# Two query-weight loads moved to SyncE's queue, one MLP copy moved to VectorE, ScalarE's small operations held back by a stricter test, and a late normalisation put ahead of a fold

## The chip, the core and the metric

One core of a Trainium2 chip runs the whole program. Its engines work side by side: TensorE (PE in the profile; PEld is its loading of weights), VectorE (DVE), ScalarE (ACT), GpSimd (POOL) and SyncE (SP). SyncE computes nothing and issues transfers; GpSimd and ScalarE issue transfers too. The transfers themselves run on 16 DMA engines. In the profile, queue q1 carries what SyncE issues, q10 what ScalarE issues and q0 what GpSimd issues; q8 and q14 bring instructions. The metric is device time in microseconds (us), lower is better.

## What is computed

A layer-normalised input of 2048 tokens and 512 channels goes through two branches, an attention with 32 heads over cached keys and values and an MLP of two stages. The attention's output, gated by the MLP's, is added to the input:

```python
xn = _layernorm(x, axis=-1)
s = _A_ref(xn, A_k_cache, A_v_cache, A_wq, A_wo)
g = _silu(_B_ref(xn, B_w1, B_w2, B_w3, B_w4))
return x + s * g
```

`_A_ref` forms queries `x @ wq`, scores against `k_cache` (32 heads, 2048 keys, 128 channels), a softmax, the product with `v_cache`, and the product with `wo`. `_B_ref` forms `gelu(layernorm(x) @ w1)`, shifts its four channel groups by one or two tokens, multiplies by `w2`, adds `x`, and then runs `gelu(layernorm(.) @ w3) @ w4`.

## The kernel before

**Units and slots.** Attention is cut into 128 units: 8 groups of 4 heads, in each group 4 query tiles of 512 tokens, in each tile the 4 heads (`units`). A unit has 8 slots (`SPU`), and slot n of the program is slot `p = n % 8` of unit `u = n // 8`. In every slot TensorE makes two score products of 512 columns (`s_slot`, into `ps_s`, of which there are two buffers), ScalarE takes their exponential in one instruction of 128x1024 (L222, into `pT`), and some slots later TensorE multiplies an earlier `pT` with the values (`pv_slot`, into `ps_o`, two buffers). Four products a slot are the base load. The other products are spread over the slots: the next queries (`q_mm`, in slots 0 and 1), the output projection (`wo_mm`, slots 4 and 5), and the MLP (slots 2, 3, 6 and 7). All engines run their instructions in the order in which this loop writes them (`pin`).

**VectorE** sums each unit's exponentials (`add_first` L228, `add_next` L233), folds the sum (`fold`, L237 and L238), forms the reciprocal, and multiplies `ps_o` with it (`norm`, L305), which also frees that `ps_o` buffer. In units after `LATE` = 20 the normalisation of unit u-3 stands in slot 1 of unit u (`normed(u - 3)`). For units that are not `turned` (the first four and the last two) the fold of unit u-1 is written in slot 0 and its sum is taken by TensorE (`sums`, four one-column products); for all others it is in slot 2, and the sum goes through a DMA transpose.

**ScalarE's small operations.** A chunk of the MLP's first stage ends with a copy of `ps_m` to `pre` (L591), on ScalarE. Two copies make a pair for `gelu_pair`: two squares (L550), a polynomial on VectorE (L554), two hyperbolic tangents (L559) and a last product on VectorE (L562). Squares and tangents wait in the list `act_late`, and at most one of them is written at the end of a slot. A budget decides which: `debt[0]` grows by `SMALL` = 2.4 (in units of one product's time) for each small operation and by `EXP_OVER` = 0.2 for each slot, and shrinks by the extra products of the slot; an operation is written when `debt[0] + SMALL` is at most what the next two slots bring in extra products (`ahead`). MLP chunks run from unit 5 on; `wo_todo` is the list of output projections that are due.

**The start.** Unit 0 is done in halves (`first_tokens`): token tiles are turned by TensorE, the first queries formed, and four half-size exponentials (L513) taken, with the queries of units 1 and 2 in between. Before that the loads are written in this order: x on SyncE and ScalarE; the query weights of heads 0, 1 and 2 on GpSimd (`load_w`, 128 KB each); on SyncE the keys of head 0 in four quarters (`load_k`, a DMA transpose of 128 KB each, L173), the values of head 0 in two halves (`load_v`, 256 KB each, L183), the four quarters of head 1's keys, and then head 2's; on GpSimd the fourth query weights, four more tiles of x, and the values of head 1. A score slot p reads quarter p // 2 of its head's keys, so unit 1 (slots 8 to 15) wants its first quarter in slot 8 and its second in slot 10. All SyncE's transfers stand in one queue in order of issue.

Of the kernel before, what the change touches and what calls it, by code (L numbers as in the profile page):

```python
# [8 lines left out]
ACT = mybir.ActivationFunctionType  # L9
ALU = mybir.AluOpType  # L10
# [7 lines left out]
def kernel(  # L18
# [15 lines left out]
    nc = tc.nc  # L34
# [16 lines left out]
    HG = 4 if H % 4 == 0 else (2 if H % 2 == 0 else 1)  # L51
    NG = H // HG

    SPU = KC // 2
    LAG = 4
    KSPLIT = 4
# [6 lines left out]
    pin = tc.keep_in_program_order  # L63

    def pool(name, bufs=1, space=None, **kw):
# [22 lines left out]
        out=ident[:], in0=diag[:], scalar1=0.0, scalar2=None, op0=ALU.is_equal))  # L88
# [30 lines left out]
    debt = [0.0]  # L119
    SMALL = 2.4  # L120
    EXP_OVER = 0.2

    def mm(out, lhsT, rhs, start, stop):
        mm_count[0] += out.shape[-1] / 512
        pin(nc.tensor.matmul(out=out, lhsT=lhsT, rhs=rhs, start=start, stop=stop))  # L125
# [24 lines left out]
    LATE = 20  # L150
# [6 lines left out]
    def at(n, fn):  # L157
        todo[n].append(fn)
# [9 lines left out]
    def load_k(h, pieces):  # L168
        w = Sk // KSPLIT
        for i in pieces:  # L170
            if i == 0:
                kTs[h] = kp.tile([P, Sk], BF16, name="kT")
            pin(nc.sync.dma_start(  # L173
                out=kTs[h][:, i * w:(i + 1) * w],
                in_=A_k_cache[0, h, i * w:(i + 1) * w, :], transpose=True))

    def load_v(h, halves, eng=nc.sync):
        v = A_v_cache[0, h].rearrange("(i p j) d -> p i j d", p=P, j=KJ)
        for i in halves:
            if i == 0:  # L180
                vBs[h] = vp.tile([P, KC, Dh], BF16, name="vb")
            ks = slice(i * KSPLIT // 2, (i + 1) * KSPLIT // 2)
            pin(eng.dma_start(  # L183
                out=vBs[h].rearrange("p (i j) d -> p i j d", j=KJ)[:, ks], in_=v[:, ks]))

    def load_w(h, eng=nc.sync):
        wqs[h] = wqp.tile([P, DC, Dh], BF16, name="wq_h")
        pin(eng.dma_start(out=wqs[h][:], in_=wq_v[:, :, h * Dh:(h + 1) * Dh]))
# [42 lines left out]
    def add_next(u, i):  # L231
        a = st[u]["acc"]
        pin(nc.vector.tensor_tensor(out=a[:], in0=a[:], in1=st[u]["pT"][i][:], op=ALU.add))  # L233

    def fold(u):
        a = st[u]["acc"]
        pin(nc.vector.tensor_tensor(out=a[:, 0:2, :], in0=a[:, 0:2, :], in1=a[:, 2:4, :], op=ALU.add))  # L237
        pin(nc.vector.tensor_tensor(out=a[:, 0, :], in0=a[:, 0, :], in1=a[:, 1, :], op=ALU.add))  # L238
# [26 lines left out]
    def turned(u):  # L265
        return T0 <= u < T1
# [275 lines left out]
    mlp = {}  # L542
    act_late = deque()

    def gelu_pair(pre, dest, n):
        sq = gtp.tile([P, 2, 512], BF16, name="sq")
        f2 = "p a f -> p (a f)"

        def square(a):
            pin(nc.scalar.activation(  # L550
                out=sq[:, a, :], in_=pre[:, a, :], func=ACT.Square, scale=GELU_A ** 0.5))

        def poly():
            pin(nc.vector.scalar_tensor_tensor(  # L554
                out=sq[:].rearrange(f2), in0=sq[:].rearrange(f2), scalar=1.0,
                in1=pre[:].rearrange(f2), op0=ALU.add, op1=ALU.mult))

        def tanh(a):
            pin(nc.scalar.activation(out=sq[:, a, :], in_=sq[:, a, :], func=ACT.Tanh, scale=GELU_C))  # L559

        def last():
            pin(nc.vector.scalar_tensor_tensor(  # L562
                out=sq[:] if callable(dest) else dest, in0=sq[:], scalar=1.0, in1=pre[:],
                op0=ALU.add, op1=ALU.mult))

        def squared(n):
            square(1)
            k = soft(n + 1)
            at(k, poly)
            at(k + 2, lambda: act_late.extend((lambda n: tanh(0), tanhed)))  # L570

        def tanhed(n):
            tanh(1)
            k = soft(n + 2)
            at(k, last)
            if callable(dest):
                for a in range(2):
                    at(k + 2 + a, lambda a=a: dest(sq[:, a, :], a))

        act_late.extend((lambda n: square(0), squared))  # L580

    def gelu_chunk(lhs, rhs, j, scale, dest):
        def run(i, n):
            if i == 0:
                mlp["ps"] = psX.tile([P, 512], FP32, tag="xm", name="ps_m")
            mm(mlp["ps"][:], lhs(i), rhs(i), i == 0, i == DC - 1)
            if i == DC - 1:
                if j == 0:
                    mlp["pre"] = gtp.tile([P, 2, 512], BF16, name="pre")
                pre = mlp["pre"]  # L590
                pin(nc.scalar.activation(out=pre[:, j, :], in_=mlp["ps"][:], func=ACT.Identity,  # L591
                                         **({} if scale is None else dict(scale=scale))))
                debt[0] += SMALL
                if j == 1:
                    gelu_pair(pre, dest(), n)
        run.size = DC
        return run
# [186 lines left out]
    wo_todo = deque()  # L784

    def ahead(n):
        u, p = divmod(n, SPU)
        if p in (2, 3, 6, 7):
            return window[p % 2] if p % 2 and window else 1 if chunks and u >= W0 // 2 else 0
        if p in (4, 5) and u < 4 * HG and not wo_todo:  # L790
            return 0
        return 2
# [3 lines left out]
        ln1_load(t, eng)  # L796
    act1 = const.tile([P, 1], FP32, name="act1")
    pin(nc.scalar.activation(out=act1[:], in_=nhalf[:, 0:1], func=ACT.Identity))
    for h in range(HG - 1):
        load_w(h, nc.gpsimd)  # L800
    load_k(0, range(KSPLIT))
    load_v(0, (0, 1))
    load_k(1, range(KSPLIT))
    warm_up(WARM)
# [28 lines left out]
    for g in range(NG - 1):  # L833
        b = (g * QT + QT - 1) * HG
        for hh in range(HG):
            h = (g + 1) * HG + hh
            for i in range(KSPLIT):
                n = (b - 2 + (2 * hh + i // 2 + (hh > 0))) * SPU + (5, 7)[i % 2]
# [22 lines left out]
    def normed(u):  # L861
        norm(u)
        gg, qq, hh = units[u]
        if hh == HG - 1 and (gg, qq) in deferred:
            at((u + 4) * SPU + 4, lambda: pin(nc.sync.dma_start(out=o_d[(gg, qq)][:], in_=oTs[(gg, qq)][:])))
        elif hh == HG - 1:
            wo_todo.extend((gg, 4 * qq + ts) for ts in range(4))
            if gg == NG - 1:
                fin_load(4 * qq)

    for n in range(NS):
        u, p = divmod(n, SPU)
# [23 lines left out]
            turned_sums(u - 2)  # L896
        if p == 0 and u >= 1:
            add_next(u - 1, 3)
            if not turned(u - 1):
                fold(u - 1)  # L900
        if p == (1 if mlp.get("stage") == 2 or u >= QUIET else 2) and HG < u < NU - 2:
            q_copy(u + 2)
# [3 lines left out]
            acc_turn(u - 1)  # L906
        if p == 1 and u > LATE:
            normed(u - 3)
        if p == (3 if u >= LATE else 2) and u >= 2 and turned(u - 2):
            bcast(u - 2)  # L910
        if n in norms:
# [44 lines left out]
            fn()  # L956
        x = mm_count[0] - mm_before - 4
        debt[0] = max(0.0, debt[0] + EXP_OVER - x) if n >= HALF else 0.0
        if act_late and debt[0] + SMALL <= ahead(n + 1) + ahead(n + 2):
            act_late.popleft()(n)  # L960
            debt[0] += SMALL
        if p == SPU - 1 and u >= 2 and turned(u - 2) and (u < LATE or u == NU - 1):
# [57 lines left out]
    for i, queue in enumerate((nc.sync, nc.scalar)):  # L1020
        cs = slice(i * D // 2, (i + 1) * D // 2)
        ps = halves[i][:, cs]
# [36 lines left out]
```

## Time and profile before

| | us |
|---|---|
| three runs: median (lowest to highest) | 1247.22 (1245.70 to 1248.73) |
| the profiled execution: its own time | 1247.53 |
| the profiled execution: its span | 1245.7 |
| TensorE busy | 1232.4 (99%) |
| ScalarE busy | 1129.2 (91%) |
| VectorE busy | 1116.5 (90%) |
| GpSimd busy | 174.6 (14%) |
| exponentials of 128x1024 (L222), each | 1.029 |
| copies `pre<-ps_m` with a scale (L591), median of 16 | 0.69 |

The span runs from the first instruction to the last; the execution's own time is 1.8 us longer, for what lies around it. A product of 512 columns is listed with 0.38 us, but products are pipelined and follow each other at 0.22 us, so TensorE's busy share tells only where it stood still for longer than that overlap. "Idle before" counts time in which an engine did nothing, and the arrow names what ended it. In the table of windows "x" counts the instructions that began in the stretch, and the DMA share is the mean over 16 engines. A few records of products are missing from the trace.

### The profile page before, as it was taken

The page shows a single profiled execution, that of the slowest core. Times are in us where ns is not written, and L with a number is a line of the kernel's source. Part 1 is how long each engine was busy: PE and PEld are TensorE (multiplying, and loading weights), DVE is VectorE, ACT ScalarE, POOL GpSimd, SP SyncE. Part 2 cuts the span into 40 slices and gives each one's busy share as a digit, 9 for nine tenths or more (in the row PEclk, how much of TensorE's full clock was granted, in tenths as well). Part 3 has the DMA queues.
Part 4 walks back from the last instruction along what each step waited for, and adds up shares of the span by engine and source line. Part 5 has one row for each costly group of instructions (what it writes and reads, how often), then busy time and mean ns, then how long its engine had stood idle before and what let it go on. Part 6 is the DMA issues. An engine that isn't in the chain of part 4 may idle for free.

```text
span 1245.7 us, 16531 instructions
## 1 busy us (share of the span) xinstructions
PE 1232.4 (99%) x5702; PEld 597.1 (48%) x5816; DVE 1116.5 (90%) x1520; ACT 1129.2 (91%) x1285; POOL 174.6 (14%) x301
## 2 busy tenths in 40 slices
PE   8999999999999999999999999999999999999998
PEld 5444444444444444444444444444444444444444
DVE  6999999999999988899988889999888999888998
ACT  8999999888999888899988889998888999988992
POOL 6563003432111000000100000010000000000110
PEclk9999999999999999999999999999999999999999
DMA  9565573665634455233484235734446233563464
GB/s 196 127 112 105 98 145 76 127 132 113 143 72 106 110 102 119 48 95 75 104 151 93 68 77 108 134 75 84 85 98 127 56 89 65 123 144 74 105 146 113
DMA packets 248404, 131.42 MB, mean 105 GB/s; under 512 B 200000, under 2 KB 224960, under 8 KB 248320
## 3 DMA queue, kind: packets, MB, share of 16 engines
q1 hardware_dynamic: 238752, 103.94, 40.1%
q0 software_dynamic: 8992, 25.96, 9.4%
q8 instruction: 45, 0.74, 0.3%
q14 instruction: 39, 0.32, 0.1%
q10 hardware_dynamic: 576, 0.46, 0.1%
HBM read 83.62 MB, written 8.13 MB: 74 GB/s over the span
## 4 chain that ended last, share of the span: by engine, by line
PE 93%; DVE 3%; DMA 2%; ACT 1%; SPq 1%; issue 1%; DVEq 0%; ACTq 0%
PE ps_o L125 34%; PE ps_s L125 33%; PE ps_m L125 10%; PE ps_q L125 8%; PE ps_wo L125 8%; DMA kT<-in_A_k_cache_dram 1%; ACT pT L222 1%; DVE acc L233 1%; SPq L173 0%; DVE acc L228 0%; DVE oT L305 0%; DMA rb<-dr 0%; DMA wo<-in_A_wo_dram 0%; DVE acc L237 0%; DVE bn L414 0%
## 5 line engine op out<-in xcount | busy, mean ns | idle before, releaser
L222 ACT ACTIVATE pT<-ps_s 128x1024 bf16<-128x1024 f32 x1020 | 1017.9, 1029 | 90.8 <-PE ps_s L125 75.0
L125 PE MATMUL ps_o<-pT,vb 128*128 128x512 bf16 x2027 | 602.9, 379 | 3.8 <-DVE oT L305 0.2
L125 PE MATMUL ps_s<-qT,kT 128*128 128x512 bf16 (+1 forms) x1992 | 595.3, 378 | 3.3 <-DMA kT<-in_A_k_cache_dram 1.8
L125 PEld LDWEIGHTS <-kT 128*128 128x128 bf16 x2056 | 232.5, 113 | 228.5 <-DMA kT<-in_A_k_cache_dram 2.5
L233 DVE TENSOR_TENSOR acc<-acc,pT 128x2048 bf16<-128x2048 bf16 x256 | 310.5, 1213 | 15.1 <-ACT pT L222 13.7
L125 PEld LDWEIGHTS <-vb 128*128 128x128 bf16 x2048 | 200.3, 98 | 225.8 <-issue 0.5
L228 DVE TENSOR_TENSOR acc<-pT 128x2048 bf16<-128x2048 bf16 x128 | 156.2, 1220 | 31.1 <-ACT pT L222 30.6
L125 PE MATMUL ps_q<-xnT,wq_h 128*128 128x512 bf16 (+1 forms) x517 | 151.3, 374 | 0.5
L125 PE MATMUL ps_wo<-wo_h,oT 128*128 128x512 bf16 (+1 forms) x453 | 133.6, 377 | 0.2
L305 DVE TENSOR_TENSOR oT<-ps_o,rb 128x512 bf16<-128x512 f32 x122 | 130.9, 1073 | 2.9 <-DMA rb<-dr 2.7
L391 DVE TENSOR_TENSOR s_acc<-ps_wo,s_acc 128x512 f32<-128x512 f32 x96 | 66.0, 688 | 41.1 <-PE ps_wo L125 40.4
L237 DVE TENSOR_TENSOR acc<-acc 128x1024 bf16<-128x1024 bf16 x128 | 87.5, 683 | 0.3
L276 DVE TENSOR_REDUCE sm<-accT 128x4 f32<-128x512 bf16 x122 | 82.7, 678 | 2.6 <-DMA accT<-acc 2.6
L125 PEld LDWEIGHTS <-wq_h 128*128 128x128 bf16 x524 | 50.7, 98 | 59.5 <-issue 0.4
L208 DVE CAST qT<-ps_q 128x512 bf16<-128x512 f32 x109 | 75.0, 688 | 3.2 <-PE ps_q L125 2.9
L125 PE MATMUL ps_m<-xn2T,w_sb 128*128 128x512 bf16 x218 | 75.3, 379 | 0.1
L125 PE MATMUL ps_m<-w_sb,h2T 128*128 128x512 bf16 x218 | 75.3, 379 | 0.1
L723 POOL DMA_DIRECT2D w_sb<-in_B_w_dram x28 | 21.2, 756 | 371.9 <-PE ps_m L125 309.9
L125 PEld LDWEIGHTS <-oT 128*128 128x128 bf16 x468 | 45.7, 98 | 54.5 <-DVE oT L312 0.3
L751 POOL DMA_DIRECT2D g_d<-xr x16 | 8.8, 548 | 438.2 <-DVE xr L749 438.2
L238 DVE TENSOR_TENSOR acc<-acc 128x512 bf16<-128x512 bf16 x128 | 54.4, 425 | 4.4
L554 DVE SCALAR_TENSOR_TENSOR sq<-sq,pre 128x1024 bf16<-128x1024 bf16 x36 | 44.0, 1222 | 4.7 <-ACT sq L550 4.6
(102 smaller groups left out, 635.3 us busy)
## 6 DMA issues: line engine op xcount, KB each, us to landing
rb<-dr SPq DMA_DIRECT2D x127, 256.0 KB, 3.8
vb<-in_A_v_cache_dram SPq DMA_DIRECT2D x60, 256.0 KB, 3.9
w_sb<-in_B_w_dram POOLq DMA_DIRECT2D x28, 256.0 KB, 4.2
wo_h<-in_A_wo_dram SPq DMA_DIRECT2D x32, 128.0 KB, 3.5
wq_h<-in_A_wq_dram SPq DMA_DIRECT2D x28, 128.0 KB, 3.2
kT<-in_A_k_cache_dram SPq DMA_TRANSPOSE x128, 3.7
dr<-rc SPq DMA_DIRECT2D x128, 2.0 KB, 2.2
xr<-in_A_x_dram POOLq DMA_DIRECT2D x16, 128.0 KB, 3.1
```

Source lines behind the costliest of these rows:

```text
L125: pin(nc.tensor.matmul(out=out, lhsT=lhsT, rhs=rhs, start=start, stop=stop))
L208: pin(nc.vector.tensor_copy(out=qT[:], in_=st[u].pop("psq")[:]))
L222: pin(nc.scalar.activation(out=s["pT"][-1][:, jj:jj + 2, :], in_=sps[:], func=ACT.Exp, scale=SCALE))
L228: pin(nc.vector.tensor_tensor(out=s["acc"][:], in0=s["pT"][0][:], in1=s["pT"][1][:], op=ALU.add))
L233: pin(nc.vector.tensor_tensor(out=a[:], in0=a[:], in1=st[u]["pT"][i][:], op=ALU.add))
L237: pin(nc.vector.tensor_tensor(out=a[:, 0:2, :], in0=a[:, 0:2, :], in1=a[:, 2:4, :], op=ALU.add))
L238: pin(nc.vector.tensor_tensor(out=a[:, 0, :], in0=a[:, 0, :], in1=a[:, 1, :], op=ALU.add))
L276: pin(nc.vector.tensor_reduce(out=sm[:], in_=s.pop("at")[:], axis=mybir.AxisListType.X, op=ALU.add))
L305: pin(nc.vector.tensor_tensor(out=oTs[(g, qt)][:, hh, :].rearrange(f, j=4), in0=s["o"].rearrange(f, j=4), in1=s["rb"].rearrange("x (p j) - ...
L391: pin(nc.vector.tensor_tensor(out=sa, in0=ps[:], in1=sa, op=ALU.add))
L554: pin(nc.vector.scalar_tensor_tensor(out=sq[:].rearrange(f2), in0=sq[:].rearrange(f2), scalar=1.0, in1=pre[:].rearrange(f2), op0=ALU.add, ...
L723: pin(nc.gpsimd.dma_start(out=w[:], in_=w3_v[:, :, fc * P:(fc + 2) * P]))
```

## The change

Four edits, in the program's order of lines.

```diff
@@ gelu_chunk: the copy at the end of an MLP chunk
-                pin(nc.scalar.activation(out=pre[:, j, :], in_=mlp["ps"][:], func=ACT.Identity,
-                                         **({} if scale is None else dict(scale=scale))))
-                debt[0] += SMALL
+                if scale is not None and n % SPU == 3 and not wo_todo:
+                    pin(nc.vector.tensor_scalar(
+                        out=pre[:, j, :], in0=mlp["ps"][:], scalar1=scale, scalar2=None, op0=ALU.mult))
+                else:
+                    pin(nc.scalar.activation(out=pre[:, j, :], in_=mlp["ps"][:], func=ACT.Identity,
+                                             **({} if scale is None else dict(scale=scale))))
+                    debt[0] += SMALL
@@ the first loads
-    for h in range(HG - 1):
-        load_w(h, nc.gpsimd)
-    load_k(0, range(KSPLIT))
+    load_w(0, nc.gpsimd)
+    load_k(0, (0, 1))
+    for h in range(1, HG - 1):
+        load_w(h)
+        load_k(0, (h + 1,))
     load_v(0, (0, 1))
     load_k(1, range(KSPLIT))
@@ the loop over slots: slot 0
             add_next(u - 1, 3)
-            if not turned(u - 1):
+            if not turned(u - 1) and u <= LATE:
                 fold(u - 1)
@@ the loop over slots: slot 1
         if p == 1 and u > LATE:
             normed(u - 3)
+            if not turned(u - 1):
+                fold(u - 1)
@@ the loop over slots: end of a slot
-        if act_late and debt[0] + SMALL <= ahead(n + 1) + ahead(n + 2):
+        if act_late and debt[0] + SMALL + 2 * EXP_OVER <= ahead(n + 1) + ahead(n + 2):
             act_late.popleft()(n)
             debt[0] += SMALL
```

TensorE's order of instructions is the same in both programs. Of the 72 copies of `ps_m`, the condition holds for one, the copy of token tile 5 in slot 75, in unit 9; on VectorE it stands behind the fold of unit 8 and ahead of the first sum of unit 9. The stricter test moves 21 of 72 squares and 11 of 72 tangents, each by one slot; of VectorE's last products four move behind two more instructions, the others stay. The moved fold is met once, in the last unit.

**SyncE at the start.** Its rows before; `kT` are a head's keys, `vb` its values, `wq_h` query weights, `xnT` turned tokens:

```order
L408 DMA xin<-in_A_x_dram 128x512 x2
L173 DMA_TRANSPOSE kT<-in_A_k_cache_dram 128x512 x4
L183 DMA vb<-in_A_v_cache_dram 128x2x512 x2
L173 DMA_TRANSPOSE kT<-in_A_k_cache_dram 128x512 x8
L465 DMA_TRANSPOSE xnT<-xn 128x4x128
L173 DMA_TRANSPOSE kT<-in_A_k_cache_dram 128x512
```

and now:

```order
L408 DMA xin<-in_A_x_dram 128x512 x2
L173 DMA_TRANSPOSE kT<-in_A_k_cache_dram 128x512 x2
L188 DMA wq_h<-in_A_wq_dram 128x4x128
L173 DMA_TRANSPOSE kT<-in_A_k_cache_dram 128x512
L188 DMA wq_h<-in_A_wq_dram 128x4x128
L173 DMA_TRANSPOSE kT<-in_A_k_cache_dram 128x512
L183 DMA vb<-in_A_v_cache_dram 128x2x512 x2
L173 DMA_TRANSPOSE kT<-in_A_k_cache_dram 128x512 x8
L465 DMA_TRANSPOSE xnT<-xn 128x4x128
```

Two loads of 128 KB now stand ahead of the third and fourth quarter of head 0's keys, and so ahead of head 0's values and of head 1's keys (the first four of the row of eight). GpSimd's row of three such loads is now a row of one; the rest of its start is the same.

**ScalarE in slot 51 and after**, at the end of the second chunk of the MLP. Before:

```order
L591 ACTIVATE pre<-ps_m,mvA 128x512
L550 ACTIVATE sq<-pre 128x512
L222 ACTIVATE pT<-ps_s 128x1024 x3
L550 ACTIVATE sq<-pre 128x512
L222 ACTIVATE pT<-ps_s 128x1024
L591 ACTIVATE pre<-ps_m,mvA 128x512
```

and now:

```order
L595 ACTIVATE pre<-ps_m,mvA 128x512
L222 ACTIVATE pT<-ps_s 128x1024
L550 ACTIVATE sq<-pre 128x512
L222 ACTIVATE pT<-ps_s 128x1024 x2
L550 ACTIVATE sq<-pre 128x512
L222 ACTIVATE pT<-ps_s 128x1024
L595 ACTIVATE pre<-ps_m,mvA 128x512
```

A copy and a square that followed each other now have an exponential between them. The same happens in slots 63, 103, 115 and 127, and in later ones.

**VectorE in unit 127**, slots 0 to 2 (`acc` is a unit's sum of exponentials, `oT` its normalised output, `gl` and `xl` the last steps of an output tile):

```order
 L261 RECIPROCAL rc<-sm 128x4
 L233 TENSOR_TENSOR acc<-acc,pT 128x2048
-L237 TENSOR_TENSOR acc<-acc 128x1024
-L238 TENSOR_TENSOR acc<-acc 128x512
-L305 TENSOR_TENSOR oT<-ps_o,rb 128x512
+L305 TENSOR_TENSOR oT<-ps_o,rb 128x512
+L237 TENSOR_TENSOR acc<-acc 128x1024
+L238 TENSOR_TENSOR acc<-acc 128x512
 L396 SCALAR_TENSOR_TENSOR gl<-s_acc,gl 128x512
 L398 TENSOR_TENSOR xl<-gl,xl 128x512
```

The normalisation of unit 124 now stands ahead of the two folds of unit 126.

## The prediction

> **What bounds the kernel now.** I read the page first, then the windows, the waits, the chain of waits, and the timeline where those point.
>
> ```profile
> PE 1232.4 (99%) x5702; PEld 597.1 (48%) x5816; DVE 1116.5 (90%) x1520; ACT 1129.2 (91%) x1285; POOL 174.6 (14%) x301
> PE 93%; DVE 3%; DMA 2%; ACT 1%; SPq 1%; issue 1%; DVEq 0%; ACTq 0%
> ```
>
> TensorE is busy for 99% of the span and holds 93% of the chain. Its products are not changed, so only its standstills can be won or lengthened, and the windows say where they are:
>
> ```profile
> 15.00:20.00 5.00, 3.44 (x17) 1.50 (x16) 4.90 (x9) 3.99 (x5) 4.76 (x6) 1.00 0.64 111
> 100.00:150.00 50.00, 49.73 (x227) 23.75 (x231) 46.76 (x59) 49.29 (x63) 5.74 (x8) 1.00 0.54 101
> 1050.00:1100.00 50.00, 49.74 (x228) 24.01 (x232) 43.98 (x57) 46.07 (x50) 1.08 (x2) 1.00 0.55 122
> ```
>
> The columns are PE, PEld, DVE, ACT and POOL, then clock, DMA share and GB/s. From 100 us on, 231 or 232 weight loads pass in every 50 us, one per 0.216 us, at full clock: TensorE runs at its rate, and work moved on other engines changes nothing there unless it makes TensorE wait. Only 15 to 20 us shows a hole. The waits name it:
>
> ```profile
> PEld L125 <- DMA kT<-in_A_k_cache_dram: 2.5, 2, 2.1
> PE ps_s L125 <- DMA kT<-in_A_k_cache_dram: 1.8, 2, 1.6
> ```
>
> Two waits for keys, the longer 1.6 us of idle PE. The chain shows whose keys:
>
> ```profile
> 7.96 1.15 SPq L173
> 9.15 10.72 DMA kT<-in_A_k_cache_dram
> ```
>
> SyncE's issue at 7.96 is the first quarter of head 1's keys; the second, issued at 9.15, landed 10.72 us later, at 19.87. On the timeline of PE and of ACT:
>
> ```profile
> 17.76 0.59 PE L125 MATMUL ps_o<-pT,vb 128*128 128x512 bf16 x2
> 19.92 0.63 PE L125 MATMUL ps_s<-qT,kT 128*128 128x512 bf16 x2 [1.56 <-DMA kT<-in_A_k_cache_dram]
> 14.18 4.81 ACT L222 ACTIVATE pT<-ps_s 128x1024 bf16<-128x1024 f32 x5
> 20.58 1.94 ACT L222 ACTIVATE pT<-ps_s 128x1024 bf16<-128x1024 f32 x2 [1.59 <-PE ps_s L125]
> ```
>
> Two products after 17.76 the next was due at 18.19 and began at 19.92, 1.73 us late. ScalarE, with one exponential per 0.96 us behind products that need 0.86, is the slower one here; it was free at 18.99 and idle for 1.59. So 1.59 us is what the absence of this wait is worth.
>
> **The change part by part.** *Loads.* Each weight load costs SyncE one issue:
>
> ```profile
> L188 SPq DMA_DIRECT2D wq_h<-in_A_wq_dram x26: 426/526/595, 112.9 to 1044.3; - x26
> ```
>
> With the 0.04 us between issues, two take 1.13 us, so head 1's second quarter is issued at 10.28, not 9.15. Its landing after the change is in no trace. The nearest rows are the first quarter's and the second's own:
>
> ```profile
> DMA to landing us min/median/max: 6.1/6.1/6.1
> ```
>
> This is the transfer issued at 7.96: 6.1 us. With 6.1 the second quarter would land at 16.4, ahead of its use; with 10.72 at 21.0. The difference between the two is a stop of the DMA engines, seen in the window from 14 to 18 us in 40 slices:
>
> ```profile
> DMA  9999090000002000200010101010110000093909
> q0 software_dynamic: 85, 0.28, 92.3%
> q1 hardware_dynamic: 524, 0.13, 20.3%
> q8 instruction: 1, 0.02, 1.7%
> ```
>
> From 14.5 to 17.5 almost no packet starts. GpSimd's queue q0 has packets open throughout (92.3%), SyncE's q1 hardly, and one instruction fetch (q8) falls into it. TensorE's program is the same, so I expect the fetch and the stop to stay, and what is open at 14.5 to land after 17.5. What changes is how much stands behind: q0 carries 256 KB less at the start, so head 1's values on it are further by then, and q1 carries 256 KB more. The bounds are the whole wait gone, and 10.72 us counted from the later issue. The small wait ahead of it goes too if head 0's second quarter no longer shares with those loads:
>
> ```profile
> 10.54 1.02 ACT L513 ACTIVATE pT<-ps_s 128x1024 bf16<-128x1024 f32 x1 [0.26 <-PE ps_s L125]
> ```
>
> It is worth 0.26, and only if the later wait does not swallow it. So the edit lies between -1.85 (1.59 + 0.26) and +1.13. The middle is -0.4; I take **-0.6**, towards the gain, because a quarter that is open when the stop ends has fewer packets of q0 to share with. Head 1's weights are read just ahead of the exponential at 10.54; if they came 1 us late, the wait at 19.92 would take that in.
>
> *ScalarE's stricter test.* Where a copy and a square stand together, the next exponential is late and with it the free `ps_s` buffer:
>
> ```profile
> 63.13 0.63 ACT L550 ACTIVATE sq<-pre 128x512 bf16<-128x512 bf16 x1
> 63.65 1.94 ACT L222 ACTIVATE pT<-ps_s 128x1024 bf16<-128x1024 f32 x2
> 64.25 0.59 PE L125 MATMUL ps_wo<-wo_h,oT 128*128 128x512 bf16 x2
> 64.73 0.59 PE L125 MATMUL ps_s<-qT,kT 128*128 128x512 bf16 x2
> ...
> 156.29 0.59 PE L125 MATMUL ps_q<-xnT,wq_h 128*128 128x512 bf16 x2
> 156.77 0.59 PE L125 MATMUL ps_s<-qT,kT 128*128 128x512 bf16 x2
> ```
>
> Two products take 0.43, these starts lie 0.48 apart: 0.05 lost. Slots 51, 63, 103, 115 and 127 have that pair, and each is followed by one such start, the first and the last shown: 5 x 0.05 = **-0.25**. The later moves fall where the windows show TensorE at its rate, and gain nothing. What is made later is covered: all moved squares are the first of their pair, so the polynomial, which needs the second, stays; the four last products that move are read by TensorE seven or more slots on. Bounds: -0.3, and +0.25 if as many new late starts appear one slot on.
>
> *The copy on VectorE.* Slot 75:
>
> ```profile
> 91.80 0.69 ACT L591 ACTIVATE pre<-ps_m,mv 128x512 bf16<-128x512 f32 x1
> 92.38 2.84 ACT L222 ACTIVATE pT<-ps_s 128x1024 bf16<-128x1024 f32 x3
> 92.83 0.59 PE L125 MATMUL ps_o<-pT,vb 128*128 128x512 bf16 x2
> 93.45 0.59 PE L125 MATMUL ps_s<-qT,kT 128*128 128x512 bf16 x2
> 94.34 1.23 DVE L233 TENSOR_TENSOR acc<-acc,pT 128x2048 bf16<-128x2048 bf16 x1 [1.08 <-ACT pT L222]
> 90.39 0.68 DVE L208 CAST qT<-ps_q 128x512 bf16<-128x512 f32 x1
> ```
>
> Without the copy the exponential starts 0.58 earlier, and the scores start at 93.26 (92.83 + 0.43), not 93.45: **-0.19**. VectorE's copy has no row; its cast from the same kind of buffer takes 0.68. It delays the first sum behind it by some 0.6, which the idle 1.08 ahead of 94.34 takes in. Were that gone, the sums and then the normalisation would be 0.6 late: up to +0.2 after the 0.19 given up.
>
> *Fold after normalisation, last unit.*
>
> ```profile
> 1217.54 0.42 DVE L238 TENSOR_TENSOR acc<-acc 128x512 bf16<-128x512 bf16 x1
> 1217.88 1.07 DVE L305 TENSOR_TENSOR oT<-ps_o,rb 128x512 bf16<-128x512 f32 x1
> 1218.22 0.59 PE L125 MATMUL ps_s<-qT,kT 128*128 128x512 bf16 x2
> 1218.99 0.59 PE L125 MATMUL ps_o<-pT,vb 128*128 128x512 bf16 x2 [0.18 <-DVE oT L305]
> 1219.42 0.27 PE L125 MATMUL ps_sum<-ones_t,acc 128*128 128x1 bf16 x4
> L295 SPq DMA_DIRECT2D rb<-dr x1: 1299/1299/1299, 1212.0 to 1212.0; - x1
> DMA to landing us min/median/max: 4.6/4.6/4.6
> ```
>
> The product on `ps_o` was due at 1218.65 and began at 1218.99, 0.34 late, behind the normalisation that frees the buffer. Ahead of the two folds that one starts 1.07 earlier, near 1216.8; its factors, issued at 1212.0, landed after 4.6 us (the last two rows), at 1216.6, just in time. The folds then end near 1218.95, and the sum's products want them at 1219.08: close, so **-0.3** of the 0.34. Bounds -0.34 and 0.
>
> *Sum:* -0.6 - 0.25 - 0.19 - 0.3 = -1.3. The profiled execution (span 1245.7) took 1247.53, 0.3 above the median 1247.22; from it 1246.2, from the median 1245.9. I write 1246.0.
>
> **The rivals.** *A, the wait for keys goes altogether.* For it: the first quarter needed 6.1 us under the same load, and q0 is relieved. Against: the stop. -1.85 - 0.74 = -2.6, 1244.6. Chance 0.28.
>
> *B, slower: head 1's keys come later still.* They stand behind 256 KB more in SyncE's queue, and the DMA engines are slow while both queues feed them, as from 4 to 9 us:
>
> ```profile
> DMA packets 1648, 0.71 MB, mean 142 GB/s; under 512 B 1566, under 2 KB 1566, under 8 KB 1648
> ```
>
> 256 KB at 142 GB/s are 1.8 us, with the later issue up to 2.9; if the first quarter, wanted two slots earlier, meets the stop and the second comes 5 us behind it as before, some 4. After the 0.74 of the small edits: +1.1 to +3.3, 1248.3 to 1250.5. It decides from a landing after 20.6; beyond 0.2% from 23.1. Chance 0.25.
>
> [...]
>
> *C, the small edits do not do what they say:* late starts return a slot on and the sums wait for the folds; with the loads at -0.3, 1246.9. Chance 0.08.
>
> **How the numbers follow.** The forecast has 0.39, A 0.28, B 0.25, C 0.08. The forecast's own range is 1245.0 to 1247.0; the runs before spread by 1.5 to each side. The range runs from 1243.9 (A, with spread) to 1249.2 (B's middle). 0.2%, about what a measurement of this kernel can tell from no change, is 2.5 us: faster by more is some 0.7 of A and a little of the forecast, 0.25; slower by more is 0.6 of B, 0.15; the rest, 0.60, lies between.
>
> **What would show it.** In the changed kernel's trace: the wait for `kT` near 19.9 shorter and the loads right; gone, A; longer, or a new one two slots ahead of it, B. Starts at 64.7 and 156.8 that lie 0.43 behind the products before them; the one at 93.4 too; no `[... <-DVE oT L305]` near 1219 and no wait of `ps_sum`. A stop of the DMA engines that is not there at all, or a new wait in the 1000 us in which TensorE ran at its rate, would make this wrong.

## The result and the profile after

| | before | after |
|---|---|---|
| median of 10 runs each, same chip (lowest to highest), us | 1246.44 (1245.40 to 1248.73) | 1249.56 (1248.28 to 1253.40) |
| ratio with its 95% interval | | 1.0028 (1.0020 to 1.0036) |
| the profiled execution, us | 1247.53 | 1253.40 |
| its span, us | 1245.7 | 1251.6 |

The change makes the kernel 0.28% slower, above the predicted range. Rival B happened. The execution profiled after the change is the slowest of its ten, so its pieces are larger than those of a usual run; a second profile below shows how much.

The page's first row and its chain by engine, of the kernel after:

```profile
PE 1241.1 (99%) x5816; PEld 598.8 (48%) x5816; DVE 1117.1 (89%) x1521; ACT 1129.0 (90%) x1284; POOL 173.5 (14%) x299
PE 98%; DMA 1%; SPq 1%; DVE 0%; issue 0%
```

The waits (us in total, times, longest):

```profile
PE ps_s L125 <- DMA kT<-in_A_k_cache_dram: 5.1, 1, 5.1
```

One wait for keys of 5.1 us, where there were two, the longer 1.6. The chain of waits says which keys:

```profile
4.20 0.58 SPq L188
...
9.05 12.70 DMA kT<-in_A_k_cache_dram
```

The two moved loads (L188; the second is issued at 6.06) now stand in the chain of SyncE's issues, and behind them head 1's first quarter is issued at 9.05 and lands 12.70 later. Before, it was issued at 7.96 and landed after 6.1. PE's timeline:

```profile
16.15 0.59 PE L125 MATMUL ps_o<-pT,vb 128*128 128x512 bf16 x2
21.79 1.04 PE L125 MATMUL ps_s<-qT,kT 128*128 128x512 bf16 x2 [5.05 <-DMA kT<-in_A_k_cache_dram]
22.63 1.06 PE L125 MATMUL ps_o<-pT,vb 128*128 128x512 bf16 x2
```

Slot 8, which began at 16.25 before, begins at 21.79. After that two products take 0.84, not 0.43. The windows show why (the columns are as in the prediction):

```profile
15.00:20.00 5.00, 1.74 (x9) 0.62 (x6) 4.90 (x8) 2.42 (x3) 4.80 (x6) 1.00 0.66 68
20.00:25.00 5.00, 3.21 (x8) 1.21 (x9) 2.17 (x6) 1.02 (x1) 3.73 (x9) 0.57 1.13 287
25.00:30.00 5.00, 5.00 (x22) 2.17 (x21) 0.35 (x2) 3.96 (x4) 0.39 (x1) 0.75 1.02 237
```

The granted clock is 0.57 and 0.75 in the ten us that follow, in windows of 1 us 0.50 from 21 to 27; from 30 us on it is 1.00 again. The same product began at 59.94 before and at 66.43 after:

```profile
66.43 0.59 PE L125 MATMUL ps_s<-qT,kT 128*128 128x512 bf16 x2
```

These 6.5 us are 5.54 for slot 8, less the 1.73 by which slot 10 was late before, and a rest of 2.7. The low clock is large enough for this rest: the two windows withhold 0.43 and 0.25 of 5 us, 3.4 us in all, a part of it while TensorE still stood (an estimate). The last product ends 5.5 us later, so the rest of the program gave some 0.9 back. Places of the small edits, in order: the pair in slot 51, the pair in slot 127, the last unit:

```profile
70.75 0.59 PE L125 MATMUL ps_wo<-wo_h,oT 128*128 128x512 bf16 x2
71.18 0.59 PE L125 MATMUL ps_s<-qT,kT 128*128 128x512 bf16 x2
...
162.39 0.59 PE L125 MATMUL ps_q<-xnT,wq_h 128*128 128x512 bf16 x2
162.82 0.59 PE L125 MATMUL ps_s<-qT,kT 128*128 128x512 bf16 x2
...
1224.52 0.59 PE L125 MATMUL ps_o<-pT,vb 128*128 128x512 bf16 x2
1224.95 0.28 PE L125 MATMUL ps_sum<-ones_t,acc 128*128 128x1 bf16 x4
```

The scores start 0.43 behind the products before them, not 0.48, and the last unit has no wait for `oT`. The small edits do what they were said to do; the loss is at the start.

### The profile page after: what moved, and what is told of

Read it like the earlier page. It is cut to its first block, busy times and chain, and to the rows that moved or that the text cites. A ratio compares the mean times of both kernels' runs of the same rounds, so it can differ in the third digit from the quotient of the medians.

```text
span 1251.6 us, 16646 instructions
## 1 busy us (share of the span) xinstructions
PE 1241.1 (99%) x5816; PEld 598.8 (48%) x5816; DVE 1117.1 (89%) x1521; ACT 1129.0 (90%) x1284; POOL 173.5 (14%) x299
## 3 DMA queue, kind: packets, MB, share of 16 engines
q1 hardware_dynamic: 239808, 104.20, 40.5%
q0 software_dynamic: 8896, 25.70, 9.3%
## 4 chain that ended last, share of the span: by engine, by line
PE 98%; DMA 1%; SPq 1%; DVE 0%; issue 0%
PE ps_s L125 36%; PE ps_o L125 35%; PE ps_m L125 10%; PE ps_q L125 9%; PE ps_wo L125 8%; DMA kT<-in_A_k_cache_dram 1%; SPq L173 0%; SPq L188 0%; SPq L183 0%; SPq L408 0%; PE ps_sum L125 0%; DVE gf L368 0%; DVE xf L373 0%
## 5 line engine op out<-in xcount | busy, mean ns | idle before, releaser
L125 PE MATMUL ps_s<-qT,kT 128*128 128x512 bf16 (+1 forms) x2056 | 610.6, 379 | 5.1 <-DMA kT<-in_A_k_cache_dram 5.1
```

## The experiments

A 95% interval stands behind every ratio to the kernel before, which ran beside each group of kernels on the same chip. The groups ran on different chips, and there the kernel before has medians from 1245.8 to 1247.8, so two ratios compare well only within a group: e1 to e4, e5 to e8, e9 to e12, e13 alone, e14 and e15.

### Which edit

**The loads alone**, and **all but the loads**:

```diff
# e1: the kernel before, with
+    load_w(0, nc.gpsimd)
+    load_k(0, (0, 1))
+    for h in range(1, HG - 1):
+        load_w(h)
+        load_k(0, (h + 1,))
# e2: the changed kernel, with
+    for h in range(HG - 1):
+        load_w(h, nc.gpsimd)
+    load_k(0, range(KSPLIT))
```

> The kernel before with the edit of the loads alone: head 1's and 2's query weights on SyncE. If the loads carry the whole loss and the small edits a gain of about 0.9 us, as the two traces suggest, this is slower than before by 4 us or more in the median (ratio 1.003 or above), with a wait of TensorE for head 1's first key quarter in slot 8. If the loss were in the small edits, this would be within 0.1% of before.

> The changed kernel with the loads put back on GpSimd: the copy on VectorE, the stricter test and the late fold alone. If the loads carry the loss: faster than before by 0.7 to 1.0 us (ratio about 0.9993), the starts at slots 51 to 127 and at the last normalisation on time, and the wait for head 1's second quarter near 19.9 as before. If the small edits carry part of the loss: slower than before.

Loads alone: 1250.22, ratio 1.0020 (1.0011 to 1.0029). All but the loads: 1246.60, ratio 0.9993 (0.9984 to 1.0002). The loss belongs to the loads. In the trace of all but the loads TensorE waits for no key of head 1; the wait near 19.9 that was expected there is missing. In the trace of the loads alone, on PE's timeline:

```profile
18.17 0.62 PE L125 MATMUL ps_s<-qT,kT 128*128 128x512 bf16 x2 [1.89 <-DMA kT<-in_A_k_cache_dram]
20.62 0.62 PE L125 MATMUL ps_s<-qT,kT 128*128 128x512 bf16 x2 [0.32 <-DMA kT<-in_A_k_cache_dram]
34.05 0.59 PE L125 MATMUL ps_q<-xnT,wq_h 128*128 128x512 bf16 x2 [1.18 <-DVE acc L233]
```

Slot 8 and slot 10 both wait for keys, and later a query product is late; the last row names VectorE, but the waits of the same trace put 1.6 us of idle of the weight loads to the turned tokens, which SyncE brings too:

```profile
PEld L125 <- DMA xnT<-xn: 1.6, 1, 1.6
```

### One execution or the program

Both kernels were profiled a second time, unchanged.

> The kernel before, unchanged, for a second profile of its start. If landings are set by the program, head 1's first quarter lands near 14.1 and its second near 19.9 again; if one execution differs from the next, the second lands anywhere from 16 to 20 (16.5 and 17.9 were seen with the loads in their old place) and the wait of 1.6 us in slot 10 is there in some executions only. Time 1245 to 1249.

> The changed kernel, unchanged, for a second profile of its start. If the landing at 21.75 is the program's, slot 8 waits about 5 us again; if it is one draw of a spread, the first quarter lands between 15.7 and 21.8 (as in the experiments that keep the loads on SyncE) and the second at 20 or later, with slot 8 or slot 10 late by 2 us or more. Time 1247 to 1254.

Before: 1245.61, span 1243.8, and no wait for keys at all. The first quarter landed 5.4 us after its issue and the second 8.0 (10.7 in the first profile). After: 1247.11, span 1245.3, and

```profile
18.28 0.62 PE L125 MATMUL ps_s<-qT,kT 128*128 128x512 bf16 x2 [1.73 <-DMA kT<-in_A_k_cache_dram]
```

So the landings differ from one execution to the next in both kernels. The wait of 1.56 us on which the prediction built its gain is there in one profile of the kernel before and not in the other; the 5.05 after is the tail of a spread, and 1.73 is another draw from it. Landings of head 1's first two quarters, each the issue plus the time to landing that the trace gives. Slot 8 wants the first at 16.1 to 16.6, and slot 10, where nothing was late ahead of it, the second at 18.2 to 18.6. The last row has the two kernels e7 and e8 below, whose loads stand as after the change:

```
                                               first issued   first landed       second landed
loads on GpSimd  before, before again, all but loads  8.0    14.1, 13.4, 14.7   19.9, 17.2, 17.9
loads on SyncE   after, after again, loads alone      9.1    21.8, 18.3, 18.2   22.1, 19.7, 20.6
                 e7, e8                               9.1    15.7, 16.9         20.4, 20.4
```

With the loads on SyncE both quarters came later, but not always both too late: in e7 the first is still in time, and the second stops slot 10. All five second landings with the loads on SyncE lie behind 18.6; of the three with the loads on GpSimd, one does.

The second profile before shows one thing more. At the end, with the folds still ahead of the normalisation, no product waited for `oT`:

```profile
1217.10 0.59 PE L125 MATMUL ps_o<-pT,vb 128*128 128x512 bf16 x2
1217.53 0.27 PE L125 MATMUL ps_sum<-ones_t,acc 128*128 128x1 bf16 x4
```

The 0.34 that the last edit removes is lost in some executions only. The edit can also cost. In the trace of e6 (below), which has it, the normalisation waited 0.35 for its own factors, and the product that sums waited for the folds behind it, as rival C said:

```profile
1217.61 0.29 PE L125 MATMUL ps_sum<-ones_t,acc 128*128 128x1 bf16 x4 [0.22 <-DVE acc L238]
```

The late starts of 0.05 in the MLP are in both profiles before (63.42 here is 64.73 there) and in neither after.

### What makes the quarter late

The expectations set two theories against each other, guesses which the runs are to tell apart: that of turns, by which what GpSimd's queue has open beside the keys makes them late, and that of the queue, by which the loads ahead in SyncE's own queue do.

**The values of head 1 out of GpSimd's queue**, with the change (e3) and without its loads edit (e6):

```diff
     load_k(1, range(KSPLIT))
+    load_v(1, (0, 1))
...
-    load_v(1, (0, 1), nc.gpsimd)
```

> The changed kernel with head 1's values (512 KB) taken off GpSimd's queue and issued by SyncE behind head 1's keys. Theory of turns (the values, nearer the front of GpSimd's queue, share the DMA engines with the keys): the keys' first quarter lands by about 18 and the wait of 5 us in slot 8 shrinks to 2 or less; time at least 2.5 us under the changed kernel. Theory of the queue (two loads ahead in SyncE's own queue make the keys late): the wait stays at 4 to 5 us and the time within 1 us of the changed kernel.

> The kernel before with the three small edits, loads of weights as before, and head 1's values issued by SyncE behind head 1's keys. If head 1's values on GpSimd's queue are what holds the keys, TensorE waits for no key of head 1 and this is the fastest of all, 1.5 to 2.5 us under before. If SyncE's longer queue then delays the turned tokens of the second tile, a wait of 1 to 2 us for xnT near 31 eats most of it, and the time is as in the run with the small edits alone.

e3: 1248.35, ratio 1.0004 (0.9993 to 1.0015); e6: 1246.28, ratio 1.0006 (0.9997 to 1.0014). In e3 the first quarter landed at 16.9 and the next three within 1.1 us of it, and slot 8 waited 0.75. Later the turned tokens, which now stand behind head 1's values in SyncE's queue, came late:

```profile
16.96 0.62 PE L125 MATMUL ps_s<-qT,kT 128*128 128x512 bf16 x2 [0.75 <-DMA kT<-in_A_k_cache_dram]
32.78 0.59 PE L125 MATMUL ps_q<-xnT,wq_h 128*128 128x512 bf16 x2 [1.63 <-DMA xnT<-xn]
```

The loss at the keys is mostly gone, and the wait for tokens is new: e3 is 1.9 us under the loads alone and still 1.8 us over all but the loads (medians of the same group). The DMA queues from 14 to 18 us, of the changed kernel and then of e3 (packets, MB, time that they took as a share of 16 engines' span):

```profile
DMA  9900000020002000109090101010101009092912
q0 software_dynamic: 46, 0.17, 120.5%
q1 hardware_dynamic: 229, 0.06, 15.9%
```

```profile
q1 hardware_dynamic: 1951, 0.63, 74.8%
q0 software_dynamic: 35, 0.07, 14.4%
```

With GpSimd's tiles of x and head 1's values open on q0, SyncE's queue starts 229 packets in 4 us; with little on q0, 1951. The 229 are the far end: in the other profiles of the two kernels, of the loads alone and of all but the loads, it starts 524 to 884; in e6, without the values on q0 too, 2026. In e6, where the loads stay on GpSimd, no time is won, though 1.5 to 2.5 us were expected: there the first quarter came at 15.3, early enough, as without this move.

**GpSimd's queue kept as long** (e5; two copies of the weight loads go on GpSimd into tiles that nothing reads), **one load of the two** (e10), and **the quarter ahead of half of head 0's values** (e9):

```diff
# e5
     load_w(0, nc.gpsimd)
+    for h in range(1, HG - 1):
+        spare = gtp.tile([P, 2, 512], BF16, name="sq")
+        pin(nc.gpsimd.dma_start(out=spare[:, 0, :].rearrange("p (c d) -> p c d", c=DC),
+                                in_=wq_v[:, :, h * Dh:(h + 1) * Dh]))
# e10
+    load_w(1, nc.gpsimd)
+    load_k(0, (0, 1, 2))
+    load_w(2)
+    load_k(0, (3,))
# e9
+    load_v(0, (0,))
+    load_k(1, (0,))
+    load_v(0, (1,))
+    load_k(1, range(1, KSPLIT))
```

> The changed kernel, and GpSimd loads the weights of heads 1 and 2 as well, into tiles that nothing reads: GpSimd's queue as long as before the change, SyncE's as long as after it, 256 KB more in all. Theory of the queue: the wait for head 1's first quarter stays or grows, time as the changed kernel or up to 2 us slower. Theory of turns (x and head 1's values come nearer and meet the keys): with that queue long again the first quarter lands before 17, the loss shrinks to 1 us or less.

> The changed kernel with only head 2's query weights on SyncE; head 1's stay on GpSimd. 128 KB instead of 256 KB are new ahead of head 1's keys. Theory of the queue: half the delay; the first quarter lands at 15 to 18, and the ratio lies between that of the small edits alone (0.9993) and that of the changed kernel (1.0028), near 1.001. Rival, one load's issue is not what counts but that head 1's weights or head 0's third quarter move: then it is at one of the two ends.

> The changed kernel, with the first quarter of head 1's keys issued ahead of the second half of head 0's values. The two loads stay on SyncE, so 256 KB of loads are new ahead of that quarter and 256 KB of values go behind it: as many bytes stand ahead of it as before the change. Theory of the queue (what stands ahead in SyncE's queue sets when the first quarter comes): it is issued near 8.5 and lands by 16, slot 8 starts on time, the second quarter, whose place is not changed, lands at 20 to 22 and stops slot 10 by 2 to 4 us as before the change; ratio 1.000 to 1.002, below the changed kernel's 1.0028. Rival, the second half of the values comes too late instead: a new wait of a product on `ps_o` near 17 of 1 us or more, ratio 1.002 or above. Rival, any load of SyncE's in this stretch is slowed by GpSimd's loads whatever stands ahead: the first quarter lands after 17 all the same.

e5: 1249.40, ratio 1.0026 (1.0015 to 1.0037), first quarter at 19.6, not ahead of 17: the loss stays with GpSimd's queue as long as before the change, so a shorter one is not needed for it (though 256 KB more move in all). e10: 1248.11, ratio 1.0012 (1.0004 to 1.0021), first quarter at 17.7: one load costs about half of two. e9: 1248.64, ratio 1.0017 (1.0008 to 1.0026). There the quarter landed at 17.0, not by 16, and the values that went behind it stopped TensorE instead:

```profile
14.12 0.60 PE L125 MATMUL ps_o<-pT,vb 128*128 128x512 bf16 x2 [0.78 <-DMA vb<-in_A_v_cache_dram]
20.34 0.99 PE L125 MATMUL ps_o<-pT,vb 128*128 128x512 bf16 x2 [2.38 <-DMA vb<-in_A_v_cache_dram]
```

The theory of SyncE's queue missed its landing here: with as many bytes ahead of it as before the change, the quarter took 8.5 us, against 5.4 to 6.7 then. The rival of the values' late second half has its wait, and that of GpSimd's loads its landing just after 17: in this order both are late.

**The loads on a third queue**, ScalarE's: behind the loads of GpSimd (e4), and early, right behind ScalarE's own tiles of x (e13):

```diff
# e4, ahead of the keys; e13, ahead of ScalarE's first activation
+    for h in range(1, HG - 1):
+        load_w(h, nc.scalar)
...
+    load_k(0, range(KSPLIT))
```

> The changed kernel with the weights of heads 1 and 2 issued by ScalarE, so that neither SyncE's queue is longer nor GpSimd's. ScalarE's first statistics start about 0.4 us later for the two issues. Theory of the queue: head 1's first quarter is issued at 7.96 again and lands near 14, the long wait is gone, time 2.5 us or more under the changed kernel. Theory of turns: GpSimd's queue is as short as in the changed kernel, head 1's values still meet the keys, and a wait of 3 us or more stays in slot 8 or 10.

> The changed kernel, with the query weights of heads 1 and 2 issued by ScalarE right behind its two tiles of x, ahead of its table load, where it waits for nothing. GpSimd's queue is as short as after the change, SyncE's as short as before it (head 1's first quarter is issued at 7.96 again, with no loads ahead of it). Theory of SyncE's queue (what stands ahead in it sets the landing): the first quarter lands by 15.5, slot 8 starts on time, ratio 0.999 to 1.0005. Rival, GpSimd's queue that is further on: its tiles of x and head 1's values stand beside the quarter earlier, the first quarter lands after 16.5 all the same, slot 8 waits 1 us or more, ratio 1.001 or above. Third way: the loads on ScalarE's queue slow x, the statistics and the first products come later by up to 2 us, and nothing is told of the two by the time, only by the landing counted from the issue (6 to 7 us, as before, or 8 and more).

e4: 1257.51, ratio 1.0080 (1.0067 to 1.0093). It does not tell the two theories apart: ScalarE stood until 11.00 ahead of these two issues, and the statistics behind them with it:

```profile
11.00 1.53 ACTq L188 DMA_DIRECT2D wq_h<-in_A_wq_dram  x2
12.57 0.63 ACT L420 ACTIVATE pre<-xin 128x512 bf16<-128x512 bf16 x1 [9.42 <-DMA kT<-in_A_k_cache_dram]
```

But GpSimd, which waits for those statistics, issued nothing in that time, and the first quarter, issued at 7.96, landed after only

```profile
DMA to landing us min/median/max: 3.6/3.6/3.6
```

e13: 1247.32, ratio 1.0011 (1.0002 to 1.0020). SyncE's queue is as before the change and GpSimd's as short as after it; the first quarter came 8.4 us after its issue, at 16.4, just in time, and the second at 19.6, 1.05 too late. Neither theory has this to itself. The rival said that GpSimd's tiles of x would stand beside the quarter earlier, but here GpSimd issued them 0.4 us later than before the change (8.12, not 7.69), and the first landed 6.5 us after its issue, not 5.3. So 8.4 us to landing can come from 256 KB more on ScalarE's queue, the third way, as well as from GpSimd's queue.

**Bytes or packets.** In the DMA queues from 2 to 9 us of the kernel before, q0 carries the three weight loads and q10 ScalarE's two tiles of x; in e13 the two loads are on q10 as well:

```profile
q0 software_dynamic: 144, 0.39, 44.5%
q10 hardware_dynamic: 288, 0.26, 10.8%
```

```profile
q10 hardware_dynamic: 1344, 0.52, 29.8%
```

A weight load is 48 packets from GpSimd and 528, half the difference, from ScalarE. From SyncE it is 528 too: on the pages of the whole program q1 has 239808 packets after and 238752 before, and 1024 more packets are under 512 bytes; q0 has 8896 and 8992. A tile of x, of 128 KB as well, is 144 packets from ScalarE (half of the 288). To tell the number of packets from the bytes, the loads went back to GpSimd, and SyncE got two extra loads of 128 KB at their places, into tiles that nothing reads: of rows of x, 128 runs of 1 KB (e14), and of weights (e15):

```diff
+    load_k(0, (0, 1))
+    for h in range(1, HG - 1):
+        spare = gtp.tile([P, 2, 512], BF16, name="sq")
+        pin(nc.sync.dma_start(out=spare[:, 0, :], in_=xsrc[h]))     # e14; e15: wq_v, head h
+        load_k(0, (h + 1,))
```

> The small edits alone (the three weight loads stay on GpSimd), and on SyncE, where the changed kernel has its two weight loads, two extra loads of 128 KB each of rows of x into tiles that nothing reads: 128 rows of 1 KB, where a weight load is 512 runs of 256 bytes. Theory of the bytes (256 KB more ahead in SyncE's queue is what costs): the first quarter of head 1's keys, issued near 9, lands at 16 to 20 and the ratio is 1.002 or more. Theory of the packets (it is the 512 packets of each weight load that take the queue's turns): the extra loads have a quarter as many, the first quarter lands by 15.5, slot 8 starts on time, ratio 0.999 to 1.001.

> As the run beside it, but the two extra loads are slices of the query weights, 512 packets of 256 bytes each, into tiles that nothing reads. Both theories expect a loss here: the first quarter lands at 16 to 20, slot 8 waits 1 to 4 us, ratio 1.002 to 1.004. Theory of the packets: clearly above the run beside it. Theory of the bytes: equal to it within the intervals. If neither loses, it is not what stands ahead in SyncE's queue, but GpSimd's shorter queue, that makes the quarter late.

e14: 1251.09, ratio 1.0036 (1.0023 to 1.0048). e15: 1249.28, ratio 1.0028 (1.0018 to 1.0037). The theory of the packets falls: a quarter as many cost no less. That of the bytes stands: with GpSimd's queue as before the change, 256 KB more ahead in SyncE's queue make a loss of this size. In their profiles it is not always the same wait that shows it:

```profile
20.32 0.63 PE L125 MATMUL ps_s<-qT,kT 128*128 128x512 bf16 x2 [2.07 <-DMA kT<-in_A_k_cache_dram]
```

```profile
14.83 0.60 PE L125 MATMUL ps_o<-pT,vb 128*128 128x512 bf16 x2 [1.76 <-DMA vb<-in_A_v_cache_dram]
19.38 0.62 PE L125 MATMUL ps_s<-qT,kT 128*128 128x512 bf16 x2 [1.14 <-DMA kT<-in_A_k_cache_dram]
```

In e14 (the first row) the first quarter came at 16.1, at the early end of what the theory of the bytes asked and in time, and it was the second that slot 10 waited for; in e15 head 0's values were late as well. Both runs also move 256 KB more in all, so the size of their loss is not only the queue's.

### The instruction fetch and the clock

**Fewer products ahead of the first real ones** moves the instruction fetch; **forty products on a spare buffer ahead of slot 8** keep TensorE at work while it would stand:

```diff
# e7
-    WARM = 48
+    WARM = 32
# e8, in the loop over slots
+        if n == 2 * HALF:
+            warm_up(40)
```

> The changed kernel with 32 instead of 48 warm-up products: TensorE's instruction fetch, which falls between 11 and 14 us, then comes some 16 products (3 us) later. If the stop of the DMA engines is started by that fetch, it moves too, to 15 to 17 us, and head 1's first quarter lands before it, by 16: the long wait goes. If the stop stays between 14 and 17.5 whatever the fetch does, the wait stays. [...]

> The changed kernel with 40 products of 128 columns on the identity ahead of slot 8, so that TensorE does not stand still while it waits for head 1's first quarter. They take about 2.2 us. If part of the loss is the halved clock after a long wait, the granted clock stays at 1.00 between 20 and 30 us and the time is 1 us or more under the changed kernel. If the clock plays no part, the time is equal or up to 2 us longer.

e7: 1248.78, ratio 1.0023 (1.0014 to 1.0032). The fetch, between 13.5 and 14 us in the first profile after, moved: from 2 to 18 us this trace has no packet on q8. The first quarter came at 15.7, by 16 as the theory of the fetch had it, but the second at 20.4, and slot 10 stood for 2.28:

```profile
20.44 0.62 PE L125 MATMUL ps_s<-qT,kT 128*128 128x512 bf16 x2 [2.28 <-DMA kT<-in_A_k_cache_dram]
```

So the loss does not go with the fetch. Nor is SyncE's queue fast without the fetch: from 14 to 18 us it starts 670 packets in this trace, within the 524 to 884 above. e8: 1249.79, ratio 1.0032 (1.0020 to 1.0045). The clock stays at full rate (the windows of e8):

```profile
15.00:20.00 5.00, 4.95 (x53) 3.59 (x53) 4.90 (x9) 2.98 (x4) 4.61 (x6) 1.00 1.03 178
20.00:25.00 5.00, 5.00 (x28) 2.36 (x26) 3.16 (x8) 4.94 (x6) 3.83 (x8) 1.00 1.18 277
```

But the forty products took 2.2 us (16.11 to 18.34), stand there also where the keys are early, and the time is no lower. That the clock held proves little here: the first quarter landed at 16.9, and without the products slot 8 would have stood for less than 1 us (an estimate from that landing).

No version here is faster than the kernel before by more than its interval; the small edits alone (0.9993) come nearest.

## Why the prediction was wrong

**The loads, -0.6: wrong, and the step that failed is the choice between the bounds**, "towards the gain, because a quarter that is open when the stop ends has fewer packets of q0 to share with", together with an upper bound, +1.13, that was too low. The loads alone cost 0.0020 of 1248, 2.5 us (1.4 to 3.6). Four things were wrong in it.

*The gain was one execution's.* The 1.59 us that the edit could win are in one of two profiles before and missing in the other, whose span is 1.9 us shorter; all but the loads misses the wait too. In a usual run there is less to win than the bound of -1.85 says.

*q0 was not relieved where it mattered.* The prediction said that "head 1's values on it are further by then". They were not: GpSimd issues them at the same time in both kernels, because it waits for statistics ahead of them; this row is in the trace before and in the trace after:

```profile
9.83 1.43 POOL L183 DMA_DIRECT2D vb<-in_A_v_cache_dram  x2
```

The two loads that left q0 had landed by then already (at 8.5 and 9.8 in the first profile before). The two halves of the values landed 10.2 and 10.7 us after their issue before and 11.2 both after; in the second profiles 7.7 and 8.0 before, 8.1 and 8.7 after. So these values were open beside the keys no shorter than before, and in e3, where they are not, the four quarters land within 1.1 us.

*The upper bound started from the same execution, and from the second quarter alone.* +1.13 is what the second quarter, landing at 21.0, would cost on top of the wait of that profile. It landed at 19.7 to 22.1 with the loads on SyncE, so this landing was a fair guess. But a run without that wait, with the quarter wanted at 18.2 to 18.6, pays 2.4 us or more for a landing at 21.0. And the first quarter, wanted two slots earlier, slipped too: 5.4 to 6.7 us to landing in three profiles with the loads on GpSimd, 9.1 to 12.7 in the three of the change and of its loads alone (6.6 and 7.8 in e7 and e8). Rival B named that ("if the first quarter, wanted two slots earlier, meets the stop") and priced 256 KB ahead in the queue at 1.8 to 2.9 us; e14 and e15 show that these bytes alone can make a loss of this size, and e10 that half of them make about half. B's range, 1248.3 to 1250.5, holds the result.

*The clock after the wait had no price.* In 20 to 25 us of the first profile after, with the wait of 5.05 us up to 21.79, the granted clock was 0.57, which can account for most of the 2.7 us counted above (an estimate). In the second profile, after a wait of 1.73, it stayed at 1.00.

**"I expect the fetch and the stop to stay": the stop did not.** It is there in the first profile of each kernel, and in the second of neither. The DMA slices from 14 to 18 us, before again and after again:

```profile
DMA  0002000004039293909799990100000909295999
DMA  9761192929812310209890983939979999942222
```

Keys are late after the change without it too (18.3 and 19.7 in after again), so the loss does not need the stop.

**ScalarE's stricter test -0.25 and the copy on VectorE -0.19: right.** The five late starts and that near 93.4 are gone in both profiles after. From the product at 59.94 (66.43) to the one near 655 the changed kernel is 0.63 shorter in the first pair of profiles and 0.41 in the second, for 0.44; of the 0.63, 0.19 are a delay near 636 us that the first profile before has and the second has not, so they are that execution's. The copy took 0.74 on VectorE, for the 0.68 of the cast:

```profile
98.36 0.74 DVE L592 TENSOR_SCALAR pre<-ps_m,mv 128x512 bf16<-128x512 f32 x1
```

**Fold after normalisation -0.3: right where the wait exists** (0.33 in the first pair), nothing in the second, where the kernel before did not have it, and the opposite sign in e6. The term was read from the one execution that had the wait, so its size is that execution's. The normalisation starts behind the first sum at 1222.07 and the folds follow at 1223.06, as said:

```profile
1222.07 1.07 DVE L305 TENSOR_TENSOR oT<-ps_o,rb 128x512 bf16<-128x512 f32 x1
```

Together the small edits gave 0.4 to 0.8 us in the two pairs of profiles, and 0.9 by the ratio of e2, with an interval that takes in nothing (0.9984 to 1.0002).

**What stays open:** what besides the bytes ahead in SyncE's queue makes the keys late. e14 and e15 show such bytes to be enough, though each moves 256 KB more in all; e9 and e13 have none more ahead of the first quarter, and it took 8.5 and 8.4 us all the same. No run shows how the engines choose between two queues with packets open, only how many packets SyncE's queue started: 229 with q0 at 120.5% of the engines' time, 1951 with q0 at 14.4%. What makes the engines start so few packets in some executions was not found either. They are not idle then: in the first profile after, q0's 46 packets from 14 to 18 us took 1.7 us each (120.5% of 16 engines for 4 us), in e3 its 35 took 0.26.

## What to carry to other kernels

Before pricing the absence of a wait for a transfer, look at a second profile of the same kernel: a wait of 1 or 2 us at the start may be one execution's, as the 1.56 was here. With two loads put ahead in SyncE's queue head 1's first quarter landed 9.1 to 12.7 us after its issue in three profiles, without them 5.4 to 6.7; in e7 it was in time and the second quarter late. So price such an edit at each transfer behind the loads, by when that one is wanted, and not only at the one that waits now. And taking loads off GpSimd's queue did not speed its next transfers here (11.2 us to landing, not 10.2 and 10.7): look when they are issued, and whether what is taken away was still in their way then.

## What was not expected of the hardware

**The granted clock was lower after standstills of 2.07 us and more, in five profiles.** The windows from 20 to 25 us, of the loads alone (e1), of e14 and, behind its wait, of e5; the standstills ahead are 1.89 and 2.07 in the rows above, and 2.60 in e5:

```profile
20.00:25.00 5.00, 4.68 (x26) 2.26 (x25) 2.93 (x8) 4.65 (x5) 3.82 (x8) 1.00 1.18 280
```

```profile
20.00:25.00 5.00, 4.68 (x18) 1.95 (x19) 1.54 (x5) 2.78 (x3) 3.82 (x8) 0.66 1.13 273
```

```profile
19.67 0.62 PE L125 MATMUL ps_s<-qT,kT 128*128 128x512 bf16 x2 [2.60 <-DMA kT<-in_A_k_cache_dram]
```

```profile
20.00:25.00 5.00, 4.95 (x16) 1.95 (x16) 2.16 (x6) 3.25 (x4) 3.73 (x9) 0.66 0.99 237
```

After standstills of 1.56 (before), 1.73 (after again) and 1.89 us (e1) the granted clock is 1.00 in this stretch; after 2.07 (e14), 2.28 (e7), 2.38 (e9) and 2.60 (e5) it is 0.66 or 0.67, which over 5 us withholds some 1.7 us of full speed (an estimate from these windows). It seems to fall in most executions of the changed kernel: their mean clock is 0.997 to 0.999 in seven of ten, while that of the kernel before is below 1.000 in 7 of its 100 executions beside the experiments.

**The same transfer of 128 KB, head 1's first quarter, took 3.6 to 12.7 us to land**, the least in e4, where GpSimd, waiting for statistics, issued nothing beside it.
